# Routing the last blocks before the early rows: a reordered end of the attention stage in a fused attention and expert kernel

## The chip, the cores and the metric

The kernel runs on one core of one Trainium2 chip. The metric is the device time of one execution in microseconds (us); the number of a kernel is the median of its timed runs. Five engines work side by side, each through its own queue of instructions and in its order: PE (TensorE, matmuls; PEld is its weight load), DVE (VectorE), ACT (ScalarE), POOL (GpSimd) and SP (SyncE, which only issues transfers here). They meet through semaphores. A queue's own instructions (register loads, branches, waits) are marked with a q behind the engine: PEldq, DVEq, SPq.

## The reference

Two blocks, both in f32. The first is a chunked attention over q, k, v of 4 batches, 8 heads, 768 positions of 64 columns: a chunk of 32 positions sees itself, 16 positions to its left, 8 to its right and 8 memory keys, by softmax. Its output is laid out as x of 3072 tokens by 512 columns. The second is a layer of 8 experts without dropped tokens: logits = x @ w_gate, each token goes to its largest logit's expert, gets y = relu(x @ w1[e]) @ w2[e] with w1 512 by 1024 and w2 1024 by 512, and y is scaled by the token's softmax weight.

## The kernel before

**Attention stage.** The 32 blocks of 96 tokens (i = 0 to 31) go through a loop written out by hand (`ordinary`, L1135 to L1190): scores of block i, then the values of block i-1 (`values`, L709: eight matmul instructions per half of the heads, then a reciprocal and a multiplication on DVE, "the division"), then the turn of block i-2 (`turn_xb`, four transposes on PE and a copy on ACT). Blocks are routed in eight groups, the last two being blocks 26 to 28 and 29 to 31. Routing a group (`routed`, L769) takes logits on PE, six small DVE steps to the chosen expert, additions of running counts on POOL (`seen`), three DVE steps to the gate, two matmuls (`rank`, L799) and three DVE steps to the row number `dest`; then POOL scatters each block's rows into a buffer in DRAM, `x_dram`, ordered by expert (`scatter_one`, L850). A scatter is put `behind` the last PE instruction issued before it.

**Early rows.** The first 256 rows of expert 0 are complete before the routing ends. They are loaded from `x_dram` at i = 29, turned on DVE (`turn_early`, L1083) and put through the first layer in eight pieces `first(f)` (L1088 to L1098: four chunks, eight matmul instructions of 256 columns, then a relu on ACT into `h0`). `part_of` (L1102) then begins their second layer: columns 0 to 255 of the first 128 rows in two parts of eight instructions, columns 256 to 383 in one of sixteen. `do_early(n)` issues the next n pieces; they stand between the routing steps of the last blocks (L1192 to L1256) and give PE work there.

**Count and barrier.** `count_up` (L971) multiplies the counts out on PE and works out on DVE each expert's first row and width (`cases`, `bases`), a flag `good` (row counts fit, and no sum of the attention was out of bounds; that part comes from `check_sums`, L901, through `okn`), and the rows to gather. Every engine then loads `good` into a register (L1253), and all meet at the barrier before the part of the experts (waits at L1914 and L1994): SP waits there for the transfers that are still under way, the others wait for SP. PE also loads the index of expert 0's code (L1242) and jumps to the next page of its instructions (`addr_align`, L1255).

**Experts.** Behind the barrier, `interlude(0)` (L1688) lets DVE make sums of expert 0's weights, loads its rows from `x_dram`, and has PE finish the early rows: columns 384 to 511 of the first 128 rows, then all 512 columns of the other 128 rows, sixteen instructions each. Then comes expert 0's first product (`sum_p<-xsT,w`), and the eight experts one after the other.

The tile that receives expert 1's `w2` lies where the turned blocks `xTs` lie, so its load (L1049, 2 MB) waits for the last logits.

Of the kernel before, what the change touches and what calls it, by code (L numbers as in the profile page):

```python
# [10 lines left out]
F32 = mybir.dt.float32  # L11
# [3 lines left out]
OP = mybir.AluOpType  # L15
# [7 lines left out]
QB = 96  # L23
NQB = S // QB
NB = B * NQB
# [58 lines left out]
EARLY_COLUMNS = 384  # L84
# [446 lines left out]
def ordinary(ctx, tc, q, k, v, mem_k, mem_v, moe_w_gate, moe_w1, moe_w2, out, good):  # L531
# [180 lines left out]
    def values(i, g, bank):  # L712
        s = st[i]
        if g == 0:
            s["x"] = xr[:, i % NXR, LB:DX]
        o = bank[0:QB, 0 : 4 * (D + 1)].rearrange("p (h d) -> p h d", h=4)
        for j in range(4):
            h = 4 * g + j
            mm(o[:, j], lhsT=s["ex"][:, h], rhs=s["v"][:, h, 0 : D + 1], start=True, stop=True)

        inv = inv_all[:, i, 4 * g : 4 * g + 4]
        nc.vector.reciprocal(inv, o[:, :, D])  # L722
        x = s["x"].rearrange("p (h d) -> p h d", h=H)
        nc.vector.tensor_tensor(x[:, 4 * g : 4 * g + 4], o[:, :, 0:D], bc(inv, 2, D), op=OP.mult)
# [246 lines left out]
    def count_up():  # L971

        cnt = cur["bank"][:, 4 * (D + 1) + 8 * E : 4 * (D + 1) + 9 * E + 1]
        mm(cnt[:, 0:E], lhsT=ones[0:QB], rhs=seen[:, NB], start=True, stop=True)
        mm(cnt[:, E : E + 1], lhsT=ones[0:QB], rhs=okn, start=True, stop=True)
        nc.vector.tensor_tensor(count, cnt[:, 0:E], ebase, op=OP.subtract)
# [28 lines left out]

        most = cpool.tile([128, 4], F32, name="most")
# [5 lines left out]
        nc.vector.tensor_scalar(most[:, 1:2], cnt[:, E : E + 1], float(QB * 2 * NB * H), None, op0=OP.is_equal)  # L1012
# [43 lines left out]
    early_ops = []  # L1056
# [6 lines left out]
    def second_layer(py, g, fs, sl=slice(0, DM)):  # L1063
        made = []
        for f in fs:
            made.append(
                mm(
                    py,
                    lhsT=h0[:, f, 128 * g : 128 * g + 128],
                    rhs=ms[0]["w2"][:, f, sl],  # L1070
                    start=f == 0,
                    stop=f == F // 128 - 1,
                )
            )
        return made[0], made[-1]

    def early_out(g, py, sl=slice(0, DM)):
        return nc.scalar.activation(early["y", g][:, sl], py, AF.Copy, scale=lab0[:, g, 1:2])

    def early_rows():  # L1080

        x0T = e0pool.tile([128, DM // 128, NER], F32, name="x0T")
        def turn_early():  # L1083
            nc.vector.transpose(
                x0T.rearrange("p k (b j) -> p k b j", j=32), x0.rearrange("p b (k i) -> p k b i", k=4)
            )

        def first(f):  # L1088
            ph = ps_s.tile([128, 2, 512], F32, tag="s", name="ph0")[:, 0, 0:NER]
            for c in range(DM // 128):  # L1090
# [9 lines left out]
        hold = {}  # L1100

        def part_of(fs, sl):  # L1102
            if fs[0] == 0:
                hold["y"] = ps_s.tile([128, 2, 512], F32, tag="s", name="py0")
            py = hold["y"][:, 0, 0 : sl.stop - sl.start]
            second_layer(py, 0, fs, sl)
            if fs[-1] == F // 128 - 1:
                early_out(0, py, sl)

        early_ops.append(turn_early)  # L1110
        for f in range(F // 128):
            early_ops.append(lambda f=f: first(f))
# [8 lines left out]
    with tc.manual_schedule():  # L1121
# [19 lines left out]
        for i in range(NB):  # L1141
# [13 lines left out]
            if i >= 1:  # L1155
                values(i - 1, 0, banks[0])
# [4 lines left out]
            if i >= 1:  # L1161
                values(i - 1, 1, banks[1])
            if late:
                place_logits(*late)
            if i > 23:
                routing(1, "p")
# [25 lines left out]
        do_early(1)  # L1192
        n = NB

        def bank_pair():
            banks = [ps_o.tile([128, 512], F32, tag="o", name="o") for _ in range(2)]
            cur["bank"] = banks[0]
            return banks
# [25 lines left out]
        banks = bank_pair()  # L1224
        late = last_logits(n - 1, banks[1])
        nc.vector.tensor_copy(*late)
        fetch_piece(1)
        work.extend(routed(len(GROUPS) - 1))
        routing(99)
        check_sums()  # L1230
        do_early(2)
        scatter_some(1)
        routing(1, "p")
        routing(99, "v")
        hold_back()
        do_early(1)
        scatter_some(1)
        count_up()
# [5 lines left out]
        while spread:  # L1244
            scatter_some(1)
            if len(early_ops) == 2:
                load_index(0)
            do_early(1)
# [3 lines left out]
        assert len(early_ops) == len(index) == 1  # L1252
# [3 lines left out]
        do_early(1)  # L1256
# [431 lines left out]
    def interlude(e):  # L1688

        before = ("before", e)  # L1690
        if e == 0:
# [10 lines left out]
            rest_of = slice(EARLY_COLUMNS, DM)  # L1702
            last = Z[:, 1, 0 : DM - EARLY_COLUMNS]
# [295 lines left out]
```

## Time and profile before

| | |
|---|---|
| median of 3 runs | 487.16 us (486.11 to 491.51) |
| profiled execution | 487.96 us, of which the span from first to last instruction 486.2 us |
| PE busy | 453.8 us (93% of the span) |
| PEld, DVE, ACT, POOL busy | 87%, 61%, 44%, 29% |
| granted TensorE clock, mean | 0.988 of 2.4 GHz |
| last value matmuls of the attention stage | 137.8 to 141.1 us |
| barrier | PE idle 163.6 to 166.6 us |
| first product of expert 0 | from 177.15 us |

Times inside the profile are counted from the span's start. A busy PE is not a PE at its peak: its rows are those of pipelined matmuls. What an engine waited for is inferred from semaphores and stands in brackets behind an idle time.

### The profile page before, as it was taken

The numbers are of one execution on the slowest core, as the hardware profiler recorded it, in microseconds if no ns is written. First come the engines' busy times: TensorE is split into PE (matmuls) and PEld (weight loads), VectorE is DVE, ScalarE is ACT, GpSimd is POOL, SyncE is SP. The second block draws the span as 40 slices with busy tenths as digits, with TensorE's granted clock in tenths as the row PEclk, the third lists the DMA queues.
The fourth block names the chain that finished last, engine by engine and source line by source line (L and its number), as shares of the span: only waits on it lengthen the run. The fifth ranks groups of instructions, "written<-read, shape, count | busy, mean of one in ns | idle before, by whom it ended". The sixth has DMA issues, their size and how long they took to land. (4 is left out here: it accounts for less than half of the span.)

```text
span 486.2 us, 9227 instructions
## 1 busy us (share of the span) xinstructions
PE 453.8 (93%) x3132; PEld 420.6 (87%) x3132; DVE 294.3 (61%) x562; ACT 215.1 (44%) x404; POOL 140.4 (29%) x191
## 2 busy tenths in 40 slices
PE   4899999999999799999899999899999998979992
PEld 4899999999998669998899899777889998869991
DVE  4466676677555557975474877744538874646410
ACT  3666666675632137214354255234234551144421
POOL 2000223323453216531352152222122243040124
PEclk9999999999999899999999999999999999989997
DMA  9999999999896485677969736935915399553002
GB/s 196 170 193 236 195 251 244 252 257 287 246 283 223 129 261 153 179 158 224 285 151 281 199 86 193 318 76 119 337 55 122 96 294 278 123 213 91 24 23 89
DMA packets 142229, 92.26 MB, mean 190 GB/s; under 512 B 79621, under 2 KB 125134, under 8 KB 142160
## 3 DMA queue, kind: packets, MB, share of 16 engines
q1 hardware_dynamic: 133744, 77.13, 63.3%
q0 software_dynamic: 6912, 13.54, 8.3%
q10 hardware_dynamic: 1504, 0.66, 0.6%
q8 instruction: 44, 0.72, 0.6%
q14 instruction: 25, 0.20, 0.1%
HBM read 65.68 MB, written 21.28 MB: 179 GB/s over the span
## 5 line engine op out<-in xcount | busy, mean ns | idle before, releaser
L1485 POOL DMA_INDIRECT out_dram<-y,lab x41 | 43.9, 1071 | 120.2 <-ACT kept L1398 62.2
L938 POOL DMA_INDIRECT lab<-x_dram,rows x42 | 50.4, 1199 | 70.6 <-PE sum_p L537 29.0
L537 PE MATMUL sum_p<-xsT,w 128*128 128x320 f32 (+8 forms) x256 | 53.9, 356 | 1.7 <-DVE h L1445 1.7
L537 PE MATMUL o<-v,ex 128*96 128x65 f32 x512 | 52.8, 247 | 0.0
L537 PEld LDWEIGHTS o<-v,ex 128*96 128x96 f32 x512 | 50.5, 165 | 1.4 <-issue 1.3
L537 PEld LDWEIGHTS sum_p<-xsT,w 128*128 128x128 f32 x256 | 43.1, 190 | 8.1 <-issue 2.7
L537 PE MATMUL sc<-qT,kT 128*128 128x192 f32 x256 | 49.2, 337 | 0.0
L708 ACT ACTIVATE ex<-sc,cst 128x256 f32<-128x256 f32 x96 | 38.5, 471 | 15.3 <-PE sc L537 15.3
L851 POOL DMA_INDIRECT x_dram<-xr,dest x32 | 29.6, 926 | 50.8 <-PE o L537 34.3
L537 PE MATMUL sum_q<-t,s 128*128 128x144 f32 (+5 forms) x192 | 37.1, 342 | 5.7 <-DVE w L1395 3.0
L659 ACT COPY qT<-tqk 64x384 f32<-64x384 f32 x60 | 30.0, 499 | 27.7 <-PE tqk L542 27.4
L537 PEld LDWEIGHTS sc<-qT,kT 128*128 128x128 f32 x256 | 42.1, 195 | 0.0
L1398 ACT COPY sum_r<-sum_p 128x640 f32<-128x640 f32 x36 | 24.4, 677 | 38.6 <-PE sum_p L537 38.6
L537 PE MATMUL sum_p<-t,s 128*128 128x144 f32 (+5 forms) x192 | 37.5, 344 | 3.4 <-ACT sum_r L1398 3.4
L537 PEld LDWEIGHTS sum_q<-t,s 128*128 128x128 f32 x192 | 31.8, 193 | 9.8 <-DVE h L1445 3.6
L677 DVE COPY kT<-tqk 64x384 f32<-64x384 f32 x60 | 33.1, 552 | 10.2 <-PE tqk L542 9.6
L537 PEld LDWEIGHTS sum_p<-t,s 128*128 128x128 f32 x192 | 32.2, 194 | 6.1 <-issue 3.8
L537 PE MATMUL sum_r<-t,w 128*128 128x144 f32 (+5 forms) x192 | 37.0, 340 | 0.0
L537 PE MATMUL sum_p<-h,w 128*128 128x144 f32 (+5 forms) x192 | 35.9, 340 | 0.5 <-ACT kept L1398 0.5
L537 PEld LDWEIGHTS sum_p<-h,w 128*128 128x128 f32 x192 | 32.0, 195 | 2.9 <-DVE xsT L1416 0.7
L537 PEld LDWEIGHTS sum_r<-t,w 128*128 128x128 f32 x192 | 32.0, 193 | 2.2
L722 DVE RECIPROCAL inv_all<-o 96x4 f32<-96x4 f32 x64 | 11.3, 176 | 35.7 <-PE o L537 35.3
(189 smaller groups left out, 795.0 us busy)
## 6 DMA issues: line engine op xcount, KB each, us to landing
w<-in_moe_w_dram SPq DMA_DIRECT2D x128, 128.0 KB, 9.1
w<-in_moe_w_dram SPq DMA_DIRECT2D x7, 2048.0 KB, 10.6
xs<-x_dram SPq DMA_DIRECT2D x56, 160.0 KB
y<-h SPq DMA_DIRECT2D x112, 80.0 KB
kn<-in_k_dram SPq DMA_DIRECT2D x16, 384.0 KB
qn<-in_q_dram SPq DMA_DIRECT2D x16, 384.0 KB
x_dram<-zeros SPq DMA_DIRECT2D x8, 396.0 KB, 3.8
v<-in_v_dram SPq DMA_DIRECT2D x24, 128.0 KB
```

The lines of the kernel that those rows point to most:

```text
L537: i = nc.tensor.matmul(*args, **more)
L659: copy(to[:, :, :, t], tq[D * t : D * t + D])
L677: i = copy(to, of[:, :, 0:PAIRS].rearrange("d a (y z p) -> d a y z p", y=2, z=2))
L708: nc.scalar.activation(ex4[:, :, :, sl], sc4[:, :, :, sl], AF.Exp, bias=mask[:, 3 * x + g : 3 * x + g + 1], scale=D**-0.5)
L722: nc.vector.reciprocal(inv, o[:, :, D])
L851: i = nc.gpsimd.indirect_dma_start(out=x_dram, out_offset=bass.IndirectOffsetOnAxis(ap=dest[:, t : t + 1], axis=0), in_=xr[:, t % NXR].bit ...
L938: return nc.gpsimd.indirect_dma_start(out=to.bitcast(I32), out_offset=None, in_=x_dram.rearrange("r (k c) -> (r k) c", c=LB), in_offset=ba ...
L1398: op("ACT", one_op(lambda: nc.scalar.copy(to, of)), reads, writes)
L1485: return nc.gpsimd.indirect_dma_start(out=out, out_offset=bass.IndirectOffsetOnAxis(ap=which.bitcast(I32), axis=0), in_=y, in_offset=None, ...
```

## The change

Only the order and the cut of the work from block 31 to the first product of expert 0 change; the arithmetic is the same.

- In the loop's last turn the logits of group 6 are taken off PSUM before the division of block 30's second half, and `turn_early` comes right behind that division instead of behind the loop.
- Behind the loop the logits of blocks 29, 30 and 31 follow each other closely, with only two half pieces of the first layer between them; both groups are ranked before the third piece, where three whole pieces and more stood between before.
- The first layer's pieces are halved (two chunks, four instructions each), on two PSUM tiles named `sides` in turn; the other banks of these tiles hold logits, ranks and the `sound` sum.
- `count_up` becomes a generator in three parts: the count's matmul; everything up to `bases`, and `check_sums` behind it; then the `sound` matmul, `good` and the rows.
- `part_of` and EARLY_COLUMNS go: the second layer of the first 128 early rows is wholly behind the barrier, with 512 columns.
- The page jump (`addr_align`) moves from the end to the middle of the pieces, behind the first half of piece 4.

```diff
-            nc.scalar.activation(h0[:, f], ph, AF.Relu)
+            if part == 1:
+                nc.scalar.activation(h0[:, f], ph, AF.Relu)
...
-        early_ops.append(lambda: part_of(range(F // 256), slice(0, DM // 2)))
-        early_ops.append(lambda: part_of(range(F // 256, F // 128), slice(0, DM // 2)))
-        early_ops.append(lambda: part_of(range(F // 128), slice(DM // 2, EARLY_COLUMNS)))
+                early_ops.append(lambda f=f, part=part: first(f, part))
...
             if late:
                 place_logits(*late)
+            if i == NB - 1:
+                norm()
+                do_early(1)
...
+        sides.extend(ps_s.tile([128, 2, 512], F32, tag="s", name="ph0") for _ in range(2))
         banks = bank_pair()
-        values(n - 1, 0, banks[0])
+        norms = [values(n - 1, 0, banks[0])]
         scatter_some(1)
-        turn_xb(n - 2)
-        late = last_logits(n - 3, banks[1])
-        values(n - 1, 1, banks[1])
+        lg29 = last_logits(n - 3, sides[1][:, 1])
+        norms.append(values(n - 1, 1, banks[1]))
         scatter_some(1)
-        nc.vector.tensor_copy(*late)
-        routing(99, "v")
+        for norm in norms:
+            norm()
         fetch_w(1, 1)
         fetch_piece(4)
+        turn_xb(n - 2)
+        do_early(1)
+        nc.vector.tensor_copy(*lg29)
+        turn_xb(n - 1)
+        lg30 = last_logits(n - 2, sides[0][:, 1])
+        routing(6, "v")
+        nc.vector.tensor_copy(*lg30)
+        routing(99, "v")
         do_early(1)
         banks = bank_pair()
-        late = last_logits(n - 2, banks[1])
-        nc.vector.tensor_copy(*late)
-        do_early(1)
-        turn_xb(n - 1)
+        lg31 = last_logits(n - 1, banks[1])
+        nc.vector.tensor_copy(*lg31)
+        before_last = list(work)
+        work.clear()
+        work.extend(routed(len(GROUPS) - 1))
+        cur["bank"] = banks[0]
+        before_last.pop(0)[1]()
+        routing(6, "v")
+        for _ in range(3):
+            before_last.pop(0)[1]()
+        spread.extend(f for _, f in before_last)
+        routing(99, "v")
+        do_early(2)
         scatter_some(1)
         do_early(1)
+        scatter_some(1)
+        cur["bank"] = sides[1][:, 1]
         routing(1, "p")
+        counting = count_up(banks[0], sides[0][:, 1])
+        next(counting)
         routing(99, "v")
         hold_back()
...
         fetch_piece(1)
...
+        next(counting)
+        scatter_some(1)
+        for _ in range(2):
+            do_early(2)
+            scatter_some(1)
+        nc.tensor.addr_align(PAGE, 0, 0)
         do_early(2)
         scatter_some(1)
...
         do_early(1)
...
+        for _ in counting:
+            pass
+        do_early(2)
+        load_index(0)
...
         tc.switch_hint({mybir.EngineType.PE: index[0]}, len(arms_of(0)), "expert0")
-        nc.tensor.addr_align(PAGE, 0, 0)
-        do_early(1)
+        do_early(2)
...
-            op("PE", lambda n: second_layer(last, 0, range(F // 128), rest_of), [], ["z1"], where=before)
-            op("ACT", one_op(lambda: early_out(0, last, rest_of)), [], ["z1", "y00"])
-            snap(Z[:, 1, DM - EARLY_COLUMNS : HALF], weights[0][1][:, 0, 0 : HALF + EARLY_COLUMNS - DM], [], ["z1"])
+            op("PE", lambda n: second_layer(Z[:, 1], 0, range(F // 128)), [], ["z1"], where=before)
+            op("ACT", one_op(lambda: early_out(0, Z[:, 1])), [], ["z1", "y00"])
```

## Rows read from the trace of the kernel before

**Rows 1.** PE's instructions in order of time around the change, merged where alike follow: start us, duration us, engine, line, operation, out<-in, shape, count [idle before, and who ended it].
```profile
137.79 1.57 PE L537 MATMUL o<-v,ex 128*96 128x65 f32 x16
...
142.86 0.77 PE L537 MATMUL o<-wg,w 128*96 128x8 f32 x8
...
145.29 0.49 PE L542 MATMUL tx<-cst,xr 96*128 96x96 f32 x4
...
153.97 0.29 PE L537 MATMUL o<-seen,ones 96*128 96x8 f32 x2
...
154.34 3.70 PE L537 MATMUL ph<-x0T,w 128*128 128x256 f32 x16
157.88 5.74 PE L537 MATMUL py<-w,h 128*128 128x256 f32 x32
166.58 0.45 PE L537 MATMUL sum_r<-nought 128*128 128x320 bf16 x2 [2.97 <-issue]
166.86 10.45 PE L537 MATMUL sum_z<-w,h 128*128 128x128 f32 x32
177.15 1.14 PE L537 MATMUL sum_p<-xsT,w 128*128 128x144 f32 x8
```

**Rows 2.** The weight loads of the last sixteen interlude instructions (512 columns each), in order of time: the first single one and the last, with thirteen steps between them.
```profile
170.71 0.19 PEld L537 LDWEIGHTS sum_z<-w,h 128*128 128x128 f32 x1 [0.27 <-issue]
...
176.29 0.19 PEld L537 LDWEIGHTS sum_z<-w,h 128*128 128x128 f32 x1 [0.24 <-issue]
```

**Rows 3.** The waits at the barrier, by line and queue: count, duration in ns (min/median/max), first and last start; and what SP's wait was for (us in total, times, longest).
```profile
L1914 SPq EVENT_SEMAPHORE  x1: 3652/3652/3652, 161.4 to 161.4; - x1
...
L1994 PEldq EVENT_SEMAPHORE  x12: 51/51/3399, 161.7 to 166.2; - x12
L1994 DVEq EVENT_SEMAPHORE  x12: 49/50/1842, 163.2 to 166.1; - x12
L1994 ACTq EVENT_SEMAPHORE  x12: 38/38/1421, 163.7 to 166.0; - x12
...
SPq L1914 <- DMA x_dram<-xr,dest: 3.7, 1, 3.7
```

**Rows 4.** The scatters and transfers ahead of the barrier: POOL's and SP's rows in order of time (the last scatter, the rows of zeros behind expert 0's); the landing of the ten scatters from 138 to 162 us (min/median/max us from issue); and SP's wait for the last logits.
```profile
160.04 0.91 POOL L851 DMA_INDIRECT x_dram<-xr,dest  x1 [0.81 <-DVE at_row L1018]
...
159.93 0.38 SPq L968 DMA_DIRECT2D x_dram<-zeros  x1
...
DMA to landing us min/median/max: 4.6/5.1/6.7
...
SPq L1049 <- PE o L537: 5.0, 1, 5.0
```

**Rows 5.** DVE's instructions in order of time: the turn of the early rows, the last division, the check of the sums (first and last of three), and the count's chain (first step, last step of `bases`, `good`, last step of the rows).
```profile
139.47 1.20 DVE L1084 STREAM_TRANSPOSE x0T<-x 128x1024 f32<-128x1024 f32 x1
...
141.49 0.42 DVE L724 TENSOR_TENSOR xr<-o,inv_all 96x256 f32<-96x256 f32 x1
...
150.44 0.28 DVE L904 TENSOR_SCALAR ok<-inv_all 96x256 f32<-96x256 f32 x1
...
150.97 0.68 DVE L906 TENSOR_REDUCE okn<-ok 96x1 f32<-96x512 f32 x1
...
154.51 0.17 DVE L976 TENSOR_TENSOR count<-o,cst 128x8 f32<-128x8 f32 x1 [1.57 <-PE o L537]
...
158.59 0.15 DVE L1004 SCALAR_TENSOR_TENSOR bases<-second,first_row 128x8 int32<-128x8 f32 x1
...
159.55 0.15 DVE L1014 TENSOR_TENSOR good<-most 1x1 int32<-1x1 f32 x1
...
162.04 0.18 DVE L1029 TENSOR_SCALAR rows<-far 128x40 int32<-128x40 f32 x1
```

**Rows 6.** DVE's load of `good`, the page jump and the other branches of PE's queue (count, ns min/median/max, first and last start), PE's weight loads behind the jump, and ACT's relu of the last first-layer piece.
```profile
L1253 DVEq TENSOR_LOAD <-good x1: 799/799/799, 162.2 to 162.2; - x1
L1255 PEldq COMPARE_BRANCH  x1: 445/445/445, 161.1 to 161.1; - x1
L1922 PEldq COMPARE_BRANCH  x16: 308/1107/5013, 172.8 to 471.9; - x16
...
161.56 1.86 PEld L537 LDWEIGHTS py<-w,h 128*128 128x128 f32 x16 [0.47 <-issue]
...
158.07 0.38 ACT L1098 ACTIVATE h<-ph 128x256 f32<-128x256 f32 x1 [1.34 <-PE ph L537]
```

**Rows 7.** The granted clock (third column from the end, 1.00 is 2.4 GHz and 0.50 is 1.2 GHz) in stretches behind three idle times of PE, and the rows of two of these idle times; the third is in rows 1.
```profile
167.00:167.50 0.50, 0.50 (x5) 0.50 (x4) 0.50 (x1) 0.00 (x0) 0.50 (x2) 0.54 0.00 0
170.00:170.50 0.50, 0.50 (x3) 0.44 (x3) 0.36 (x1) 0.50 (x2) 0.00 (x0) 0.55 1.15 329
...
233.08 1.70 PE L537 MATMUL sum_q<-t,s 128*128 128x216 f32 x8 [2.99 <-DVE w L1395]
233.00:236.00 3.00, 2.92 (x16) 2.95 (x17) 0.35 (x1) 0.69 (x1) 2.39 (x3) 1.00 0.95 264
...
428.71 2.52 PE L537 MATMUL sum_p<-t,s 128*128 128x248 f32 x8 [3.44 <-ACT sum_r L1398]
430.00:430.50 0.50, 0.50 (x2) 0.42 (x2) 0.50 (x2) 0.00 (x0) 0.50 (x1) 0.50 1.06 414
```

**Rows 8.** DVE behind the barrier: the turns of expert 0's rows, which the first product and the sums read.
```profile
172.13 1.84 DVE L1416 STREAM_TRANSPOSE xsT<-xs 128x768 f32<-128x768 f32 x2 [1.76 <-DMA xs<-x_dram]
```

More of the change, by code (lines that the diff above doesn't have):

```diff
@@ L83 @@
 PAGE = 256
-EARLY_COLUMNS = 384
 LB = 16
@@ L719, in values, with norm @@
             mm(o[:, j], lhsT=s["ex"][:, h], rhs=s["v"][:, h, 0 : D + 1], start=True, stop=True)
[L721 to L724, printed above, removed]
+        def norm():
+            inv = inv_all[:, i, 4 * g : 4 * g + 4]
+            nc.vector.reciprocal(inv, o[:, :, D])
+            x = s["x"].rearrange("p (h d) -> p h d", h=H)
+            nc.vector.tensor_tensor(x[:, 4 * g : 4 * g + 4], o[:, :, 0:D], bc(inv, 2, D), op=OP.mult)
+        return norm
     def turn_xb(i):
@@ L968, in end_rows, with count_up @@
         return nc.sync.dma_start(to, bc(zeros.bitcast(I32), 1, 2))
[L971 to L976, printed above, removed]
+    def count_up(bank, other):
+        cnt = bank[:, 4 * (D + 1) + 8 * E : 4 * (D + 1) + 9 * E]
+        mm(cnt, lhsT=ones[0:QB], rhs=seen[:, NB], start=True, stop=True)
+        yield
+        nc.vector.tensor_tensor(count, cnt, ebase, op=OP.subtract)
         nc.vector.tensor_tensor(count[:, 0:1], count[:, 0:1], n0, op=OP.subtract)
@@ L1004, in count_up @@
         nc.vector.scalar_tensor_tensor(bases[:, 1], second, 0.0, first, op0=OP.max, op1=OP.add)
+        check_sums()
+        yield
+        sound = other[:, 4 * (D + 1) + 9 * E : 4 * (D + 1) + 9 * E + 1]
+        mm(sound, lhsT=ones[0:QB], rhs=okn, start=True, stop=True)
         most = cpool.tile([128, 4], F32, name="most")
@@ L1011, in count_up @@
         nc.vector.tensor_scalar(most[:, 0:1], most[:, 0:1], float(XC), None, op0=OP.is_le)
-        nc.vector.tensor_scalar(most[:, 1:2], cnt[:, E : E + 1], float(QB * 2 * NB * H), None, op0=OP.is_equal)
+        nc.vector.tensor_scalar(most[:, 1:2], sound, float(QB * 2 * NB * H), None, op0=OP.is_equal)
         nc.vector.tensor_tensor(most[:, 0:1], most[:, 0:1], most[:, 2:3], op=OP.mult)
@@ L1075, in second_layer, with early_out @@
         return made[0], made[-1]
-    def early_out(g, py, sl=slice(0, DM)):
-        return nc.scalar.activation(early["y", g][:, sl], py, AF.Copy, scale=lab0[:, g, 1:2])
+    def early_out(g, py):
+        return nc.scalar.activation(early["y", g], py, AF.Copy, scale=lab0[:, g, 1:2])
     def early_rows():
@@ L1086, in turn_early, with first @@
             )
-        def first(f):
-            ph = ps_s.tile([128, 2, 512], F32, tag="s", name="ph0")[:, 0, 0:NER]
-            for c in range(DM // 128):
+        def first(f, part):
+            ph, half = sides[f % 2][:, 0, 0:NER], DM // 256
+            for c in range(half * part, half * part + half):
                 mm(
@@ L1097, in first @@
                 )
-            nc.scalar.activation(h0[:, f], ph, AF.Relu)
[L1100 to L1108, printed above, removed]
+            if part == 1:
+                nc.scalar.activation(h0[:, f], ph, AF.Relu)
         early_ops.append(turn_early)
         for f in range(F // 128):
-            early_ops.append(lambda f=f: first(f))
-        early_ops.append(lambda: part_of(range(F // 256), slice(0, DM // 2)))
-        early_ops.append(lambda: part_of(range(F // 256, F // 128), slice(0, DM // 2)))
-        early_ops.append(lambda: part_of(range(F // 128), slice(DM // 2, EARLY_COLUMNS)))
+            for part in range(2):
+                early_ops.append(lambda f=f, part=part: first(f, part))
     def do_early(n):
@@ L1155, in ordinary @@
             if i >= 1:
-                values(i - 1, 0, banks[0])
+                values(i - 1, 0, banks[0])()
             need(i - 2, turn_xb)
@@ L1161, in ordinary @@
             if i >= 1:
-                values(i - 1, 1, banks[1])
+                norm = values(i - 1, 1, banks[1])
+                if i < NB - 1:
+                    norm()
             if late:
                 place_logits(*late)
+            if i == NB - 1:
+                norm()
+                do_early(1)
             if i > 23:
@@ L1190, in ordinary @@
                 early_gather()
-        do_early(1)
         n = NB
         def bank_pair():
-            banks = [ps_o.tile([128, 512], F32, tag="o", name="o") for _ in range(2)]
-            cur["bank"] = banks[0]
-            return banks
+            return [ps_o.tile([128, 512], F32, tag="o", name="o") for _ in range(2)]
+        sides.extend(ps_s.tile([128, 2, 512], F32, tag="s", name="ph0") for _ in range(2))
         banks = bank_pair()
-        values(n - 1, 0, banks[0])
+        norms = [values(n - 1, 0, banks[0])]
@@ L1238, in ordinary @@
-        count_up()
         index = []
@@ L1242, in load_index @@
             index.append(nc.tensor.value_load(cases[0:1, e : e + 1], min_val=0, max_val=len(arms_of(e)) - 1))
[L1244 to L1248, printed above, removed]
+        for _ in counting:
+            pass
+        do_early(2)
+        load_index(0)
+        assert not spread, len(spread)
         zeroed = end_rows(0)
```

22 lines of the change are left out of this document (5 added, 17 removed).

## The prediction

> **What bounds the kernel now.** The page shows PE busy for 93% of the span, so a change in this stage is worth what it takes out of PE's row of work or its idle time. I read PE's rows in time order first [rows 1]. From the last values at 137.79 us to the end of the second-layer pieces (157.88 + 5.74 = 163.62) there is no idle time in brackets; then PE stands for 2.97 us until 166.58, works through the interlude for 10.57 us and begins expert 0's first product at 177.15. The idle time is the barrier. The wait view tells who opens it [rows 3]: SP waits from 161.4 for 3.65 us, to 165.05, for a scatter into `x_dram`; PE's queue, there since 161.7, is let go at 161.7 + 3.40 = 165.1, and so are DVE's (163.2 + 1.84) and ACT's (163.7 + 1.42). The last scatter was issued at 160.04 and landings here take 4.6 to 6.7 us [rows 4]: that is the releaser. From 165.05 to PE's first instruction pass another 1.53 us. The first product's operands are not what is late: DVE has turned expert 0's rows by 173.97 [rows 8], and PE is still in the interlude for 3.2 us more. So the two things that count are the barrier's time and the length of the interlude on PE.
>
> **What moves from before the barrier to behind it.** Thirty-two instructions (5.74 us) leave the front of the barrier [rows 1]. Behind it, the sixteen of 128 columns become sixteen of 512. The price of those is on show: the second early half has the same shape, and its steps are (176.29 - 170.71) / 13 = 0.43 us [rows 2], so 16 x 0.43 = 6.88 us. The new interlude on PE is 0.28 (its opening, 166.58 to 166.86) + 6.88 + 6.88 = 14.04 us at full clock, against 10.57 today: 3.47 us longer. The old one includes a slow stretch: from about 167.0 to 170.45 the granted clock is 0.50 [rows 7], in which the sixteen small ones took 10.45 - 6.88 = 3.57 us. ACT's copy-out grows likewise, but stands while PE works on the second half: nothing.
>
> **The new order up to the barrier, PE.** Values, three logits, turns, ranks, counts and eight pieces are the same instructions as those that fill PE from 137.79 to 157.88, in another order; halving a piece adds none. So PE would again be through by 157.9, plus new waits: the turn of block 31 needs the last division (it ended at 141.91 and now follows `turn_early` and the rest just as closely; PE gets there near 141.7, so up to 0.3), the `sound` matmul needs `okn`, and the last piece follows PE's load of `good`. Together I take 0.5: 158.4.
>
> **The count's chain.** With logits at 0.65 us (142.86 to 143.48 or so), a turn 0.33 and half a piece 0.88 (two whole ones from 154.34 to 157.88), PE has issued from 138.5: three halves and logits at 0.7 each, a turn, half a piece, a turn, logits, half a piece, logits: the last logits end near 144.5. DVE's copy and six steps and POOL's three additions take some 2.2 us, to 146.7, while PE has the rank of group 6 and a piece and a half to do, to 147.4. Then rank and count: 147.9, against 154.26 today [rows 1]. Three steps to `dest` now stand behind this on DVE (0.65), so the chain of `count` starts at 148.6 instead of 154.51: 5.9 earlier. It is 158.74 - 154.51 = 4.23 long up to `bases`, then comes the check of the sums (150.44 to 151.65: 1.2 us, moved into the chain), then `good` and the rows [rows 5]. `good` comes at 159.70 - 5.9 + 1.2 = 155.0 and the rows end at 162.22 - 4.7 = 157.5. DVE's load of `good` and two more steps put it at the barrier 1.0 us after that, as today (163.2): 158.5. PE's queue needs 1.4 us from `good` to the next piece (159.70 to the jump at 161.1), so to 156.4, while its last queued pieces run to about 156.2: the 0.2 are in the 0.5 above.
>
> **Scatters, transfers, ACT.** The last scatter stands behind the first half of piece 5, five half pieces and the `sound` sum before PE's end: 158.4 - 5 x 0.88 - 0.3 = 153.7; six at 1.22 us each from about 147.0 have just caught up. It lands 4.6 to 6.7 us later; I take 5.0, the value of the one that opens the barrier today: near 158.7. The zeros follow `bases` (152.8) by 1.2 us and landed in less than the barrier's time today; they come with the scatter at the latest. Expert 1's `w2` is held up by the last logits for 5.0 us today [rows 4]; these come 4 us earlier, so its 2 MB leave the transfers sooner and take nothing from the last scatters. ACT's last relu ends 0.4 us after PE [rows 6]: 158.9.
>
> **The page jump** costs PE's queue 0.445 us, today with PE idle for 0.47 behind it [rows 6]. In the middle of the pieces PE has instructions queued; I take nothing, with bounds of 0 and 5.0, the longest branch of that queue.
>
> **Sum.** Everyone is at the barrier by 158.9 instead of 165.05; PE starts at 160.4 instead of 166.58 (6.2 earlier) after 2.0 us idle instead of 2.97. The interlude is 3.47 longer: the first product starts 2.7 us earlier, at 174.4, if the clock stays at 2.4 GHz; its operands come 6.2 earlier as well, by 167.8, and wait. If the clock falls again, half of 3.4 us is lost: 1.7, and 1.0 us remain of the gain. PE is the bound of the experts behind, so the shift is carried to the end.
>
> **The clock** decides more than half of this. The idle times of 2.97 us (rows at 166.58) and 3.44 (428.71) were followed by 1.2 GHz, that of 2.99 at 233.08 was not [rows 7]. The new idle time, 2.0, is shorter than all three, so I lean to full clock, by less than two to one.
>
> **Rivals.** *The clock falls nonetheless* (an idle time of 2.97 was enough once): -1.0 us, 486.2. *The scatter keeps the barrier*, and ends slower: if POOL's chain of six starts late or the last one lands in 6.7 instead of 5.0, the release moves to 160.4, PE's idle time to 3.5 us, as long as those that were followed by half clock: -2.7 + 1.5 + 1.7 = +0.5; with both (another 1.5) +2.0, 489.2. It decides from a release 1.0 us later than mine if the clock falls with it. For it: scatters wait for PE and for each other; against: the transfers are quieter by then. *The jump is not covered.* Branches of PE's queue take 0.31 to 5.01 us, 1.1 in the median [rows 6]; one of 5.0 with about 1.5 queued in front of it puts PE's end 3.5 later, the barrier with it, and the idle time ahead of it is split: +0.8, 488.0; at the median, nothing. The Trainium skill (Runtime: NRT & Kernel Launch, Instruction fetch mechanics) says that a taken branch to a page which is not at hand stops the queue until that page is fetched. By that rule a jump made while the queue runs ahead could stall where today's, made after a wait for `good`, did not; today's 0.445 us shows no such fetch. *The change is off the path altogether*: PE's total work shrinks by 32 to 16 wider instructions only, and new waits of a microsecond among logits and ranks eat the rest: no difference, 487.
>
> **Numbers.** The profiled execution took 487.96 us, 0.8 above the median; the sum gives 485.2 for it and 487.16 - 2.7 = 484.5 for the median. Chances: full clock 0.42 (483.6 to 485.6), half clock 0.25 (485.6 to 486.7), late scatter 0.13 (487.3 to 489.2), jump 0.08 (487 to 488), off the path 0.08; 0.04 for a gain beyond 4 us. The range 482.8 to 487.6 leaves out the far ends of these. One per cent, 4.9 us, is about what a measurement of this kernel can tell from no change (its three runs span 1.1%). Faster by more has 0.05, slower by more (two of the rivals together) 0.04.
>
> **What would show it.** Right: the last logits near 144.5; PE idle at the barrier about 2 us, from 158.4; the first product near 174.4 with no clock below 1.00 before it, or 176.1 with. Wrong: SP's wait ending after 161, a bracket of over 0.5 us among the halved pieces, or a first product released by DVE.

## The result and the profile after

The changed kernel takes 491.03 us in the median (487.63 to 497.18), the kernel before 488.23 us (485.45 to 491.73) in runs beside it: a ratio of 1.0069, 95% interval 1.0047 to 1.0092. It is 0.7% slower; 484.5 us were forecast, with a range up to 487.6. Ratios here and below leave out runs over 1.5% above the fastest of the same kernel; medians do not. Its profiled execution took 490.04 us, with a span of 488.2 us.

PE in order of time, from the logits of group 6 (the last row whose place is the same in both orders) to the first product. Columns as in [rows 1].

```profile
137.99 0.86 PE L536 MATMUL o<-w,wg 128*32 128x96 f32 x24
...
139.97 0.87 PE L536 MATMUL o<-v,ex 128*96 128x65 f32 x8 [0.30 <-issue]
...
144.07 0.39 PE L541 MATMUL tx<-cst,xr 96*128 96x96 f32 x2 [0.47 <-DVE inv_all L722]
144.29 0.77 PE L536 MATMUL ph<-wg,w 128*96 128x8 f32 x8
145.31 1.13 PE L536 MATMUL ph<-x0T,w 128*128 128x256 f32 x4 [0.25 <-DVE lg L1217]
...
150.43 6.29 PE L536 MATMUL ph<-x0T,w 128*128 128x256 f32 x28
157.54 0.38 PE L536 MATMUL ph<-okn,ones 96*128 96x1 f32 x2 [0.83 <-ACT h L1106]
158.17 1.99 PE L536 MATMUL ph<-x0T,w 128*128 128x256 f32 x8 [0.25 <-DVE most L1019]
160.88 1.98 PE L536 MATMUL ph<-x0T,w 128*128 128x256 f32 x8 [0.71 <-ACT h L1106]
164.66 0.45 PE L536 MATMUL sum_r<-nought 128*128 128x320 bf16 x2 [1.80 <-issue]
164.94 13.90 PE L536 MATMUL sum_z<-w,h 128*128 128x512 f32 x32
178.67 1.14 PE L536 MATMUL sum_p<-xsT,w 128*128 128x144 f32 x8
```

Against [rows 1], PE starts behind the barrier 1.92 us earlier (164.66 instead of 166.58), its interlude is 3.44 us longer (14.01 instead of 10.57), and the first product comes 1.52 us later. PE's end stands at 160.88 + 1.98 = 162.86, with six brackets on the way that sum to 2.81 us; in the trace of the prediction there was none. The first of them, 0.30 us, is not the new order's alone: another profile of the kernel before (e9) has 0.27 at the same place.

The scatters' and the flag's way, from POOL, SP, DVE and PE's queue: the last scatter, the zeros, the first step of the count's chain, the last of `bases`, `good`, the last of the rows; PE's loads of the index (the first of the eight in that line) and of `good`; SP's waits at the barrier; and the relu on ACT that the `sound` sum waits for.

```profile
157.44 0.91 POOL L854 DMA_INDIRECT x_dram<-xr,dest  x1 [1.72 <-PE ph L536]
...
157.05 0.36 SPq L971 DMA_DIRECT2D x_dram<-zeros  x1
...
150.97 0.16 DVE L979 TENSOR_TENSOR count<-o,cst 128x8 f32<-128x8 f32 x1
154.77 0.16 DVE L1007 SCALAR_TENSOR_TENSOR bases<-second,first_row 128x8 int32<-128x8 f32 x1
158.22 0.15 DVE L1021 TENSOR_TENSOR good<-most 1x1 int32<-1x1 f32 x1
160.71 0.18 DVE L1036 TENSOR_SCALAR rows<-far 128x40 int32<-128x40 f32 x1
...
L1256 PEldq TENSOR_LOAD <-cases x8: 298/525/1369, 158.2 to 171.5; - x8
L1267 PEldq TENSOR_LOAD <-good x1: 637/637/637, 159.5 to 159.5; - x1
...
SPq L1924 <- ACT h L1106: 1.6, 1, 1.6
SPq L1924 <- DMA x_dram<-xr,dest: 1.6, 1, 1.6
...
157.11 0.66 ACT L1106 ACTIVATE h<-ph 128x256 f32<-128x256 f32 x2 [3.42 <-PE ph L536]
```

SP no longer waits for the scatter alone [rows 3]: half of its wait is for the last relu, that is for PE's end. The last scatter comes 2.6 us earlier than before and the count's chain 3.54 us [rows 4, 5]; `good` gains only 1.3. The bracket of 0.71 in the first fence names a relu, but PE's queue was in its two register loads from 158.2 on. The relu that the `sound` sum waited for was itself late: ACT stood for 3.42 us and then did two in a row.

The page jump, the branch of PE's queue at its new place; the granted clock around the barrier (third column from the end); and the turns of expert 0's rows.

```profile
L1249 PEldq COMPARE_BRANCH  x1: 323/323/323, 152.0 to 152.0; - x1
...
163.00:165.00 2.00, 0.34 (x3) 1.00 0.03 8
165.00:167.00 2.00, 2.00 (x6) 1.00 0.40 100
167.00:169.00 2.00, 2.00 (x6) 1.00 0.90 227
...
170.80 1.84 DVE L1429 STREAM_TRANSPOSE xsT<-xs 128x768 f32<-128x768 f32 x2 [2.50 <-DMA xs<-x_dram]
```

The jump lies within the 28 matmuls that run on from 150.43. The half clock of [rows 7] behind this barrier is gone. The operands are turned by 170.80 + 1.84 = 172.64, six microseconds before PE takes them; before, they were ready 3.2 us ahead [rows 8].

### The profile page after: what moved, and what is told of

The parts are those of the page before. It is cut to its first block, busy times and chain, and to the rows that moved or that the text cites. A ratio compares the mean times of both kernels' runs of the same rounds, so it can differ in the third digit from the quotient of the medians.

```text
span 488.2 us, 9163 instructions
## 1 busy us (share of the span) xinstructions
PE 453.6 (93%) x3100; PEld 416.1 (85%) x3100; DVE 293.7 (60%) x562; ACT 214.5 (44%) x401; POOL 140.6 (29%) x191
## 5 line engine op out<-in xcount | busy, mean ns | idle before, releaser
L707 ACT ACTIVATE ex<-sc,cst 128x256 f32<-128x256 f32 x96 | 38.6, 472 | 15.4 <-PE sc L536 13.2
L854 POOL DMA_INDIRECT x_dram<-xr,dest x32 | 29.6, 926 | 51.3 <-PE o L536 33.8
L536 PE MATMUL sum_p<-t,s 128*128 128x144 f32 (+5 forms) x192 | 38.6, 351 | 2.8 <-ACT sum_r L1411 2.8
L1408 DVE TENSOR_TENSOR h<-sum_p,kept 128x640 f32<-128x640 f32 x12 | 9.9, 824 | 39.1 <-ACT sum_r L1411 33.6
```

Of the source, the lines that this page charges most:

```text
L707: nc.scalar.activation(ex4[:, :, :, sl], sc4[:, :, :, sl], AF.Exp, bias=mask[:, 3 * x + g : 3 * x + g + 1], scale=D**-0.5)
L854: i = nc.gpsimd.indirect_dma_start(out=x_dram, out_offset=bass.IndirectOffsetOnAxis(ap=dest[:, t : t + 1], axis=0), in_=xr[:, t % NXR].bit ...
L1408: op(eng, one_op(lambda: engines[eng].tensor_tensor(out, a, b, op=how)), reads, writes, upto=upto)
```

## The experiments

Three theories stood against each other. **A**: the loss is PE's waits among the halved pieces. **B**: it is the second layer, 3.5 us more of it behind the barrier than the barrier gives back. **C**: it is stretches in which several engines stand, which the change doesn't make.

All kernels are compared in one table further down, on one measure: the time from the start of the logits of group 6 to the first product, called **the stage** here. The zero of each row is the start of its row `o<-w,wg` x24 (137.99 in the changed kernel; 137.00 in the trace of the prediction). Runs e1 to e4, e5 to e8, e9 to e12 and e13 to e16 were each made on a chip of their own, beside runs of the kernel before on that chip; a ratio holds for its chip. The forecast in this measure: PE's end 21.4, first instruction behind the barrier 23.4, first product 37.4; the trace before: 26.6, 29.6 and 40.15.

### e1, e2: each of two waits taken away

e1 puts logits, rank and `sound` sum on PSUM tiles that no piece uses:

```diff
-        lg30 = last_logits(n - 2, sides[0][:, 1])
+        lg30 = last_logits(n - 2, banks[1])
...
-        cur["bank"] = sides[1][:, 1]
+        cur["bank"] = banks[1]
...
-        counting = count_up(banks[0], sides[0][:, 1])
+        counting = count_up(banks[0], banks[1])
```

> The changed kernel, but the logits of block 30, the rank of the last group and the sound sum write into the banks that held the values, so that the two side tiles hold nothing but the first layer's pieces. Theory A (the loss is PE's waits among the pieces: 0.25 us for the logits of block 30, 0.83 for sound behind a relu of piece 4, 0.25 behind the read of sound): these brackets go, PE is through 1.3 us earlier, and the kernel is about 1.3 us faster than the changed one, still 1 to 2 us slower than before. Theory B (the loss is the second layer behind the barrier, 3.5 us more of it, which an earlier barrier would have to give back): the brackets go, too, but the barrier moves less than 1 us, since the load of good and the last piece set it, and the time stays within 0.7 us of the changed kernel's. Theory C (chance standstills of all engines at once, seen in the one profile near 100, 139 and 156 us): the brackets may be there or not, the time is that of the changed kernel.

e2 puts PE's register loads behind the last piece:

```diff
         for _ in counting:
             pass
-        do_early(2)
+        do_early(4)
         load_index(0)
...
         tc.switch_hint({mybir.EngineType.PE: index[0]}, len(arms_of(0)), "expert0")
-        do_early(2)
```

> The changed kernel, but PE gets the last piece ahead of its loads of expert 0's index and of good, not behind them. Theory A: the 0.71 us in which PE stood ahead of the last piece go; the loads run beside the piece, the barrier opens about 0.7 us earlier and the kernel is 0.7 us faster than the changed one. Theory B: the same 0.7 us at most, as it leaves the second layer where it is. Theory C: nothing. If PE's queue rather than its array is last at the barrier, the loads behind the piece cost the barrier what the piece gained: no difference.

Measured: e1 486.73 us, ratio to before 1.0027 (0.9994 to 1.006); e2 486.55 us, 1.0017 (0.998 to 1.0054). PE in e1, from the `sound` sum on:

```profile
154.57 0.28 PE L536 MATMUL o<-okn,ones 96*128 96x1 f32 x2
154.71 1.97 PE L536 MATMUL ph<-x0T,w 128*128 128x256 f32 x8
157.07 1.99 PE L536 MATMUL ph<-x0T,w 128*128 128x256 f32 x8 [0.38 <-issue]
161.64 0.45 PE L536 MATMUL sum_r<-nought 128*128 128x320 bf16 x2 [2.59 <-issue]
161.93 13.90 PE L536 MATMUL sum_z<-w,h 128*128 128x512 f32 x32
175.66 1.14 PE L536 MATMUL sum_p<-xsT,w 128*128 128x144 f32 x8
```

The waits for relu, logits and `most` (the step that reads the `sound` sum) are gone, and a bracket of 0.38 us at the loads is left. PE's end comes 21.5 us into the stage, which is the forecast; in e2, 21.6. In e2 the two brackets of 0.25 us stand as in the changed kernel, PE is idle for 3.08 us at the barrier and then works at half clock until 165.3. Neither kernel comes out faster than before. A is right that PE's end depends on these waits, and that is not enough. But the edits do not account for the whole of it: e2 takes away the loads, 1.0 us, and its PE's end is 3.2 us earlier. e2, which leaves the tiles shared, has no wait at the `sound` sum either (154.81, no bracket), and neither has one at the turn of block 31.

### e3: the second layer in front again

The changed order, with the second-layer parts of the kernel before ahead of the barrier (three pieces more) and its narrow rest behind; PE's two register loads come to stand among these parts, behind the first layer, so that the edit of e2 is in part in it:

```diff
+        early_ops.append(lambda: part_of(range(F // 256), slice(0, DM // 2), 0))
+        early_ops.append(lambda: part_of(range(F // 256, F // 128), slice(0, DM // 2), 0))
+        early_ops.append(lambda: part_of(range(F // 128), slice(DM // 2, EARLY_COLUMNS), 1))
...
-        do_early(2)
+        do_early(5)
         load_index(0)
+        do_early(1)
...
-        do_early(2)
+        do_early(1)
```

> The changed order of the routing, but three quarters of the first early rows' second layer ahead of the barrier again, in the parts of the kernel before, behind the last piece. Theory B: the interlude on PE is back at about 10.5 us, PE's idle time at the barrier falls under 2 us because the routing and the scatters are done long before, and the time is that of the kernel before or up to 1.5 us less. Theory A: PE's waits of about 2.3 us among the pieces stay, PE reaches the barrier 2 us later than in the kernel before, and the kernel is 1 to 3 us slower than before, as the changed one is. Theory C: as the changed kernel.

Measured: 484.47 us, ratio 0.9967 (0.9931 to 1.0003). The brackets behind the logits of block 30 and behind the `sound` sum stand (0.26 and 0.25 us), and yet the stage is 37.4 us. PE has matmuls up to 26.9 and is idle for 1.60 us.

### e4: the old order with the second layer behind the barrier

```diff
-        early_ops.append(lambda: part_of(range(F // 256), slice(0, DM // 2)))
-        early_ops.append(lambda: part_of(range(F // 256, F // 128), slice(0, DM // 2)))
-        early_ops.append(lambda: part_of(range(F // 128), slice(DM // 2, EARLY_COLUMNS)))
```

> The kernel before with one part of the change alone: the whole second layer of the first early rows goes behind the barrier, the routing keeps its old order. Theory B: the interlude is 14 us, the barrier opens hardly earlier (DVE's chain ends at 162.2 and its load of good at 163.2, against the scatter's 165.05), so that the kernel is 1.5 to 3.5 us slower than before, about what the changed kernel is. Theory A: PE's second layer only changes sides of the barrier and its idle time, and the kernel is within 1 us of before. Theory C: within 1 us of before.

Measured: 488.62 to 497.57 us in six runs, the two lowest 488.62 and 492.42, with a median of 486.17 before, beside it. The six are too few for a ratio; even the lowest is above that median. PE in e4:

```profile
161.20 3.78 PE L537 MATMUL ph<-x0T,w 128*128 128x256 f32 x8 [5.28 <-DVE far L1026]
166.59 0.72 PE L537 MATMUL sum_r<-nought 128*128 128x320 bf16 x2 [1.61 <-issue]
167.10 15.62 PE L537 MATMUL sum_z<-w,h 128*128 128x512 f32 x32
```

Without the second layer nothing is left to run while PE's queue waits for `good`: 5.28 us idle, half clock up to 170.6, and the stage is 45.9. What stood ahead of the barrier was the cover of that wait.

### e5 to e8: the changed kernel again, both mends, the best of both, the jump

> The changed kernel as it is, beside the same runs of the kernel before as the next three. If the waits among the pieces cost what its profile shows (theory A: brackets of 2.81 us on PE between the last values and its end), it stands about 0.5% behind the two kernels that take one of them away, and the ratio to before is near 1.006 again. If its 0.7% came from the stretches in which several engines stood (theory C: 0.98 us in the attention stage, and more behind), a new profile shows other gaps, and the ratio can come out anywhere from 0.998 to 1.009. Theory B (3.5 us of second layer behind the barrier) makes no difference between this and the kernels of the first experiments.

Measured: 490.43 us, ratio 1.0051 (1.0007 to 1.0094). The brackets are there again (1.12, 0.25, 0.65, 0.25, 0.75 us), and so is the stage, 40.72 us after 40.68.

e6 makes the edits of e1 and e2 together:

> Both mends of the first two experiments in one: logits, rank and sound sum off the tiles of the pieces, and both register loads of PE behind the last piece. Theory A: no bracket over 0.3 us on PE from the last values to its end; PE's end about 158.5, SP let go by the last scatter at about 160.3, PE idle 2.5 to 3.1 us because both loads stand there; time about as e1, 0.998 to 1.003 of before. Theory B: no faster than e1 or e2, since what is left is the interlude of 13.9 us; whichever of the two mends is made, the sum of idle time and interlude stays at 16.5 us or more. If A alone were right the ratio would be 0.994 to 0.996, the 2.7 us that were forecast.

Measured: 489.14 us, ratio 1.0027 (0.9981 to 1.0073), with a stage of 38.5 us in its profile. A wait of 0.48 us for the last division, at the turn of block 31, is left on PE. The stage gains, the median doesn't: this is what e13 to e15 had to settle.

e7 makes the edits of e1 and e3 together:

> The changed order with the second-layer parts of before ahead of the barrier again, and logits, rank and sound sum on banks of their own. Theory B: at least as fast as e3, 0.994 to 0.997 of before, with PE busy up to about 163.5, idle below 2 us, an interlude of 8.8 to 10.6 us and the first product at 174 to 176. Theory A adds 0.8 to 1.3 us to what e3 gained (PE's brackets at the rank and the sound sum go): 0.992 to 0.995. Were the order of the routing worth nothing, it would come out at 1.000.

Measured: 486.46 us, ratio 0.9965 (0.9929 to 1.0), with before at 488.66 us. Beside e5, on the same chip, the intervals do not meet; beside e6 they overlap by a hair (0.9981 to 1.0). Its ratio is that of e3, so the 0.5 us of brackets in e3 can't be seen at this width. The `sound` sum and the piece behind it in e7, and the relu of that time:

```profile
156.52 0.28 PE L537 MATMUL o<-okn,ones 96*128 96x1 f32 x2
157.36 3.72 PE L537 MATMUL ph<-x0T,w 128*128 128x256 f32 x16 [0.56 <-issue]
...
156.92 0.66 ACT L1107 ACTIVATE h<-ph 128x256 f32<-128x256 f32 x2 [3.27 <-PE o L537]
```

ACT is as late as in the changed kernel. On a bank of its own the `sound` sum does not wait for the relu, but the piece behind it stands for 0.56 us.

e8 is the changed kernel with `addr_align` moved back between the load of `good` and the last two half pieces:

> The changed kernel with the page jump at its old place, between the load of good and the last two half pieces. If the jump in mid-queue is covered, as its profile shows (323 ns at 152.0 with matmuls running on), this is 0 to 0.5 us slower than the changed kernel: 0.45 us more on PE ahead of the last two half pieces. If the jump amid queued pieces costs something that the profile puts elsewhere, this is faster than the changed kernel by more than 0.5 us. The ratio to before, from theory A, 1.005 to 1.009.

Measured: 490.57 us, ratio 1.0019 (0.9968 to 1.0069). The interval overlaps that of e5, so the place of the jump makes no difference that can be seen. In its profile the bracket ahead of the last half pieces is 1.21 us instead of 0.68 to 0.75, the 0.45 expected for a jump that nothing covers.

### e9 to e12: the kernel before and the changed kernel, profiled again

> The kernel before, profiled again. The forecast counted 1.7 us as won because the half clock behind the barrier (167.0 to 170.5 us) was to go with the shorter idle time. If that stretch belongs to the kernel before, it is there again: interlude of sum_z 10.4 us, last values to first product 36.8 us. If it is chance, the sixteen small and sixteen wide ones take 8.8 us at 1.00, and from the last values to the first product it is about 35.0 us, as short as in e6.

> A third profile of the kernel before, for the same question: 36.8 us from the last values to the first product if the clock falls behind its barrier as a rule, 35.0 if not. Two of three without the fall would mean that the forecast priced the gain on one profile's chance.

> A fourth profile of the kernel before, for the same question: 36.8 or 35.0 us from the last values to the first product.

These expectations count from the last values, which start 2.9 to 3.9 us behind the stage's zero. Measured from there: 37.3, 37.2 and 38.4 us. The half clock belongs to the kernel before: it stands behind its barrier in all four profiles, and the stage is 40.15, 41.16, 41.01 and 42.25 us. PE's idle time, 2.97 us in the trace of the prediction, is 3.41 to 3.47 in the others. So the forecast did not rest on one profile's chance here: the fall that it hoped to avoid is there each time.

> A third profile of the changed kernel. Theory A: the brackets of 0.25 us at the rank's and the sound sum's successor, of 0.6 to 0.8 us at the sound sum and of 0.7 us ahead of the last two half pieces stand there again, since they come from the order written out, and last values to first product take 37.3 to 37.9 us at full clock. Theory C: they are gone or elsewhere, and the stage takes 35 to 36 us.

The brackets are there as A had them, at the `sound` sum only 0.32 us, and half clock stands at a new place, which neither theory expected; from the last values to the first product it takes 40.7 us. PE's windows in e12 (start:end, length, PE busy, granted clock third from the end):

```profile
142.00:144.00 2.00, 0.81 (x11) 1.00 0.97 320
144.00:146.00 2.00, 1.74 (x8) 0.65 0.93 336
146.00:148.00 2.00, 2.00 (x13) 0.50 0.36 144
```

PE, which waits 1.19 us for the turn of block 31 here, is busy for 0.81 us of two, and half clock stands from 144.6 to 151.4. e8 shows the like from 146.3 to 149.8; the first two profiles of the changed kernel do not. The stage is 43.5 us here.

### e13 to e16: where the gain of the mended kernels goes

Three more profiles of e6's kernel and one more of e7's.

> The kernel of e6, profiled again. If its stage is short every time: 38.1 to 38.6 us from the logits of group 6 to the first product, no half clock behind the barrier, and what it lacks in the median stands as half clock elsewhere. If e6's short stage was chance: 40 us or more.

> The kernel of e6, a third profile: 38.1 to 38.6 us if the short stage belongs to it, 40 us or more (half clock behind the barrier or among the pieces) if it does not.

> The kernel of e6, a fourth profile, as the two ahead of it: 38.1 to 38.6 us, or 40 us and more.

e6's short stage was the chance: these take 39.96, 42.76 and 39.93 us (e14 with waits of 0.53 and 0.86 us of its own among the pieces). PE in e13; its windows behind the end; and the last scatter's time to landing in e15 (us from issue):

```profile
147.08 6.29 PE L536 MATMUL ph<-x0T,w 128*128 128x256 f32 x28
153.21 0.28 PE L536 MATMUL o<-okn,ones 96*128 96x1 f32 x2
153.35 3.70 PE L536 MATMUL ph<-x0T,w 128*128 128x256 f32 x16
160.49 0.69 PE L536 MATMUL sum_r<-nought 128*128 128x320 bf16 x2 [3.44 <-issue]
160.97 15.39 PE L536 MATMUL sum_z<-w,h 128*128 128x512 f32 x32
176.20 1.14 PE L536 MATMUL sum_p<-xsT,w 128*128 128x144 f32 x8
...
157.00:160.00 3.00, 0.05 (x1) 1.00 0.05 19
160.00:162.00 2.00, 1.51 (x4) 0.64 0.08 17
162.00:164.00 2.00, 2.00 (x4) 0.51 0.90 237
```

```profile
L854 POOL DMA_INDIRECT x_dram<-xr,dest x1: 915/915/915, 152.6 to 152.6; - x1
DMA to landing us min/median/max: 5.9/5.9/5.9
```

With no wait among its pieces PE is through 20.8 us into the stage in e13 and e15, better than forecast. But the last scatter takes 5.9 us to land in e15, SP waits for it (3.1 us in e13), PE stands for 3.44 us, and the clock falls. The interlude's 32 wide instructions take 15.4 instead of 13.9 us. In e6 the last scatter came 2.5 us behind the one ahead of it, not 1.3, and SP's wait for it ended by 159.9, at most 4.3 us after its issue (155.62).

> The kernel of e7, profiled again: from the logits of group 6 to the first product 37.4 to 38.4 us, PE idle 1.6 us at the barrier, full clock behind it. If its lower median is the clock's alone, the stage is no shorter than in e13 to e15 and fewer stretches of half clock stand in the rest; if it is the second layer's place, the stage is shorter than theirs.

Measured: a stage of 36.84 us, the shortest of all. PE and its windows at the barrier:

```profile
157.01 5.40 PE L537 MATMUL ph<-w,h 128*128 128x256 f32 x32
164.19 0.45 PE L537 MATMUL sum_r<-nought 128*128 128x320 bf16 x2 [1.78 <-issue]
164.47 8.82 PE L537 MATMUL sum_z<-w,h 128*128 128x128 f32 x32
173.12 1.14 PE L537 MATMUL sum_p<-xsT,w 128*128 128x144 f32 x8
...
164.00:166.00 2.00, 1.81 (x16) 1.00 0.22 55
```

The same order up to 157 us as in e13 (20.7 us into the stage), and then 5.40 us of second layer, in which the scatter lands. PE's idle time is 1.78 us and the clock stays.

### All profiles on one measure

| kernel | profile | PE's end | PE idle at barrier | first product | half clock in the stage |
|---|---|---|---|---|---|
| before | first | 26.6 | 2.97 | 40.15 | behind barrier |
| before | e9, e10, e11 | 27.1, 27.0, 27.1 | 3.46, 3.41, 3.47 | 41.16, 41.01, 42.25 | behind barrier, each |
| changed | first, e5 | 24.9, 24.9 | 1.80, 1.80 | 40.68, 40.72 | none |
| changed | e12 | 27.9 | 1.62 | 43.53 | among the pieces |
| changed, jump last | e8 | 26.9 | 1.61 | 42.52 | among the pieces |
| own banks | e1 | 21.5 | 2.59 | 38.06 | none |
| loads last | e2 | 21.6 | 3.08 | 40.27 | behind barrier |
| both mends | e6 | 21.9 | 2.65 | 38.53 | none |
| both mends | e13, e14, e15 | 20.8, 22.6, 20.8 | 3.44, 3.47, 3.44 | 39.96, 42.76, 39.93 | behind barrier, each |
| layer in front | e3 | 26.9 | 1.60 | 37.41 | none |
| layer in front, own banks | e7, e16 | 27.8, 26.1 | 1.61, 1.78 | 38.36, 36.84 | none |
| old order, layer behind | e4 | 28.4 | 1.61 | 45.94 | from 160.3 to 170.6 us |

## Why the prediction was wrong, point by point

**The interlude** was right: 14.04 us forecast, 14.01 measured. So were **the operands** and **the page jump**: 323 ns with matmuls running on. The rule of the Trainium skill that the prediction weighed there (Runtime: NRT & Kernel Launch, Instruction fetch mechanics) has an engine stop when the page that it jumps to is not at hand; no row here shows such a stop, and e5 beside e8 shows no price.

**The clock and the idle time** behind the barrier came out as forecast (2.0 us forecast, 1.62 to 1.80 in three profiles, 1.00 granted), but by luck. PE's end and the barrier were late together. Where PE's end came as forecast, in e1 and e2, PE stood for 2.59 and 3.08 us, the second time with half clock behind it.

**The step that failed first is "Together I take 0.5"**, the term for new waits on PE. PE's end was to come 21.4 us into the stage and comes at 24.9: the waits cost 4.0 us instead of 0.5. The rows of the changed kernel against those of e13, which has none of them, say where. The lag grows by 1.2 us up to the logits of block 30 (0.5 ahead of the values of block 31, the rest at its turn), by 0.4 at the piece behind these logits, by 1.0 at the `sound` sum, by 0.5 at the piece behind it and by 1.0 at the register loads: 4.1.

About 1.9 of the 4.1 belong to the order as written. Logits, rank and `sound` sum share tiles with the pieces, and though they lie in other banks, the piece behind them waits until they are read: 0.4 and 0.5 us here, with a bracket that names the reader in every profile with shared tiles and in none with own banks. These two places were not in the forecast's list. Of the loads 1.4 us from `good` to the next piece were forecast, and 2.5 passed (158.37 to 160.88), since PE's queue has the load of the index ahead of that of `good`; e2 took this away.

The other 2.2 come and go. The logits of block 30 begin 6.3 to 6.5 us into the stage in all profiles of the changed kernel and in e8, and 5.1 in e1, e2, e3, e13, e15 and e16 (5.9 in e14). But e6 and e7 have them at 6.2, and theirs are the kernels of e13 to e15 and of e16, run on another chip; so it is not the edits that take this lag away. (The forecast had the turn with up to 0.3 us.) The `sound` sum waited for a relu and not for `okn`. That takes a shared tile and a late ACT, which stands for 2.9 to 3.4 us ahead of this relu in the changed kernel, e8 and e7, and is on time in e2 and e3. What holds the engines at these two places stays open; it may be what theory C supposed.

The way to the last logits was added up wrong in the text (138.5 and the steps listed give 145.0, not 144.5), but without the waits the result holds: in e13 they end 7.5 us into the stage, which is 144.5.

The steps behind PE's end carry its delay: chain of the count 13.0 us into the stage instead of 11.6, last scatter 19.5 instead of 16.7, `good` 20.4 instead of 18.0, PE behind the barrier 26.7 instead of 23.4. So the barrier gave 2.9 us where 6.2 were forecast, and the interlude took 3.4.

**The second step that failed is the landing, "I take 5.0".** It is 5.9 in e15, 6.0 in e2, e14 and e16 and 5.5 in e3, and not of the last one alone: the ten scatters take 6.3 us in the median in e13, 5.1 before [rows 4]. That "the transfers are quieter by then" did not make them land sooner. The changed kernel's own last scatter comes late and does not show it: it was issued at 157.44, and SP was on to its wait for the relu by 161.7. Where PE's end is as forecast or earlier, it is the rival "the scatter keeps the barrier" that stands. In e13 and e15 its price is almost right: PE idle 3.44 us (3.5 forecast), half clock, and a stage 0.2 us shorter than in the trace of the prediction, where +0.5 was forecast; in e14 the stage is 2.6 us longer. This rival had a chance of 0.13, though [rows 4] show landings of up to 6.7 us. Of the six profiles with a mend, e1 and e6 alone missed the half clock, with idle times of 2.59 and 2.65 us.

**What the change gave away** was not a term of the sum. The sum priced the moved second layer by its duration behind the barrier, and as worth nothing in front. In front it was the work that covered the scatter's landing and the load of `good`: e16 and e13 share their order up to 20.7 us into the stage, and differ by 3.1 us at the first product. In the times e7 stands clear of e5, from which it differs in banks, loads and second layer; beside e6, which lacks the second layer alone, its interval overlaps, so this price is shown in the stage and only likely in the times. Theories A and B are both true, then: A for part of PE's end, B for what a mended PE could gain. Routing the last blocks ahead is worth its effort only with that cover: e3 and e7 stand at 0.9967 and 0.9965 of before, with intervals that end at 1.0003 and 1.0, so a gain is likely and not shown. They are the fastest kernels here.

**How much slower** is explained in part. The mean span of the changed kernel's three profiles is 487.9 us and that of the four of before 486.0. Of these 1.9 us, 0.5 lie in the stage (41.64 against 41.14, with the half clock among the pieces in one of three), 0.8 ahead of it (137.85 against 137.04), where the code is the same, and 0.6 behind it. Over all profiles the part ahead of the stage runs from 136.1 to 138.9 us and the part behind from 306.1 to 310.5, whatever the kernel; whether the shares outside the stage are chance or a consequence stays open, and theory C with it. Nor do three and four profiles reach the 0.7% of the runs, 3.4 us. Stretches in which several engines stand are there in either kernel: from 99 to 103 us PE is busy for 3.50 of the 4 us in the changed kernel's first profile, for 3.63 in e9 and for 4.00 in the first of before. The rival "off the path altogether", which had new waits eat the gain, comes nearest; it ended at no difference.

## What to carry to other kernels

Work ahead of a barrier has two prices: its duration, and what it covers. Before it is moved behind the barrier, one asks what else is still on its way at that time (a scatter's landing, a register load), and whether PE would stand there and lose its clock. And small matmuls that shared a PSUM tile with a running sequence were tied to its waits here, even in another bank (0.25 us at each hand-over, more when the reader was late): they get a tile of their own.

## What the runs showed of the hardware

At this barrier PE's idle time and the clock behind it went together in every profile (e4 aside, whose clock had fallen earlier): idle times of 1.60 to 2.65 us (nine profiles) were followed by 2.4 GHz, those of 2.97 to 3.47 (eight profiles) by 1.2 GHz. In e2, e11 and e14 the clock fell while PE still stood, 0.2 to 1.4 us before its first matmul. Elsewhere it is less plain: [rows 7] have 2.99 us with no fall. The Trainium skill (TensorE: Matmul & The Clock Gate, HAM oscillation — how this bites in real kernels) describes waits for transfers that let the clock fall, so that the next matmuls start slow; e13 and e16 agree, with 15.4 us for an interlude that takes 13.9 at full clock, and none lost where matmuls fill the wait.

Over the 22 runs of the changed kernel the time goes by and large with the mean granted clock: 487.9 us at 0.993, 494.1 at 0.974, though 487.9 and 492.2 both stand at 0.988. A sum of a few microseconds is therefore read better from several profiles than from one: the stage of one kernel differed by up to 4.2 us between executions (e6 and e14, on two chips), and one profile of e6 alone would have settled the wrong answer.
